# Block transposes by a detour through HBM in a fused attention and SoLU kernel

## The chip, the cores and the metric

The kernel runs on one core of a Trainium2 chip. The metric is the device time of one execution in microseconds; less is better.

## What is computed

Windowed attention over 8 batches and 8 heads of 576 positions with 64 dimensions (a window of 32 for the first four heads, the same reach with a dilation of 4 for the others) gives 4608 rows of 512 numbers. Each row then goes through a layer of two products with a SoLU and a normalisation between them:

```
x = attn_out.transpose(0, 2, 1, 3).reshape(B * S, H * D)      # 4608 x 512
h = x @ w_in                                                  # 4608 x 1024
sm = softmax(h)
solu = h * sm
ln = (solu - mean(solu)) / sqrt(var(solu) + 1e-6) * g_ln
out = ln @ w_out                                              # 4608 x 512
```

## The kernel before

The rows are cut into 36 tiles of 128 tokens. TensorE does both products with operands that are split into a high part and a rest (x_hi and x_lo, th and tl, two parts of each weight), three matmuls for each block of 128: 24 matmuls of 512 columns for the first product of a tile (two halves of 512 columns, L296) and 24 for the second (L378). Attention is done in 32 units of two heads; a unit has scores (S, L188), a softmax on VectorE, GpSimd and ScalarE, a turn by VectorE's 32x32 transposes (L246), and attend (V, L262), whose result is spread into x_hi (ScalarE, L280) and x_lo (VectorE, L283).

For a tile i of the layer the work after the first product is: maximum (peak, VectorE, L307), exponential (e, ScalarE, L314), gate (VectorE, L321, reads the product from PSUM, multiplies with e and sums), centring (mid, VectorE, L333), squares and the scale rstd (var, ScalarE and GpSimd), and then the second product, which needs the activations with their 1024 features on the partitions. So TensorE transposes tile t in eight blocks of 128x128 into two PSUM banks (moe_t, L354), ScalarE casts them to th (L361), VectorE subtracts to get tl (L369). After the second product ScalarE writes ob from PSUM (L388) and SP stores it.

Every engine runs its instructions in the order in which they are written. After an opening that is written out by hand (weights are converted, tiles 0 to 5 of the first product, the first attention units) one loop runs over the tiles, and each step emits the words of STEP in order. A word has a name and says for which index it is meant: i is the step's tile, j the tile before, n and m the attention units of this step and the one before. Step 6 is the first of the loop; steps 12, 21 and 30 to 35 have no new attention unit.

```
STEP = "ha.i hb.i S.n q.n mask.n max.n sub.n hc.i hd.i V.m v.m peak.i exp.n sum.n
        inv.n e.i gate.i mid.i xh.m xl.m var.i norm.n turn.n o.j t.i th.i tl.i out.j"
```

PSUM has eight banks. The first product has banks 0 and 1, once, so the next tile's first product waits for this tile's gate. The second product has bank 2, once, so the next one waits for ob; scores use banks 2 and 3, the transposes 3 and 4, attend 4 to 7. SP issues all transfers: the loads of q, k and v for four units ahead and the stores of the output.

## Time and profile before

| | us |
|---|---|
| median of 3 runs | 568.08 |
| the runs | 568.32, 566.10, 568.08 |
| span of the profiled execution | 564.7 |
| TensorE busy | 529.4 |
| VectorE busy | 358.4 |
| ScalarE busy | 236.4 |
| GpSimd busy | 113.3 |

The span runs from the first to the last instruction of one execution that the profiler recorded on the core. That execution's own time is not listed apart from its span; the three runs lie 1.4 to 3.6 above it, the median 3.4. The transfers move 51.66 MB, 91 GB/s over the span. In the opening TensorE waits for loads and conversions; from about 100 us on it is never idle for long. TensorE's mean granted clock is 0.979 of full speed, and 1.00 in every stretch after the opening.

### The profile page before, as it was taken

To read this page: it belongs to the slowest core of one execution; us is meant where nothing else is said; L and a number is where in the kernel's file an instruction comes from. 1 tells how busy PE (TensorE), PEld (TensorE's weight loads), DVE (VectorE), ACT (ScalarE), POOL (GpSimd) and SP (SyncE) were. 2 spreads that over 40 slices of the span, in tenths; PEclk is the share of its full clock that TensorE was granted. 3 is DMA by queue.
4 is the path that set the end of the run, shared out by engine and by line. 5 is a ranking of instruction groups with operands and counts; after the bars stand their busy time and mean duration, and the time that the engine had idled before them with its cause. 6 is when DMAs were issued, how large, how long until landed. Compare 5 with 4: busy or idle time off the path is not lost.

```text
span 564.7 us, 16571 instructions
## 1 busy us (share of the span) xinstructions
PE 529.4 (94%) x7418; PEld 421.6 (75%) x7418; DVE 358.4 (63%) x554; ACT 236.4 (42%) x384; POOL 113.3 (20%) x258
## 2 busy tenths in 40 slices
PE   3586599999999999999999999999999999999996
PEld 2354477787888888888888888888888888888884
DVE  4778886567666667466667666476667666443431
ACT  4567964543333333433333334433333334432232
POOL 0003662122222222122222221122222221111110
PEclk9867989999999999999999999999999999999999
DMA  8975305222322222112223222123221000000000
GB/s 315 399 283 186 104 1 167 79 79 74 93 93 92 93 93 93 48 64 93 92 93 93 93 92 93 48 64 93 93 93 48 21 21 21 20 24 33 19 20 37
DMA packets 22103, 51.66 MB, mean 91 GB/s; under 512 B 2704, under 2 KB 3088, under 8 KB 22032
## 3 DMA queue, kind: packets, MB, share of 16 engines
q1 hardware_dynamic: 22032, 50.61, 26.6%
q8 instruction: 58, 0.95, 0.7%
q14 instruction: 13, 0.11, 0.1%
HBM read 41.16 MB, written 9.44 MB: 90 GB/s over the span
## 4 chain that ended last, share of the span: by engine, by line
PE 90%; DVE 4%; DMA 3%; ACT 2%; issue 1%; SPq 0%; ACTq 0%
PE banks L296 36%; PE banks L378 35%; PE banks L262 6%; PE banks L354 5%; PE banks L188 5%; PE banks L452 1%; DMA t<-w_in 1%; DMA vt<-vw 1%; DMA mask_sb<-mask 1%; DVE nmax L307 1%; DVE t L321 1%; DVE x_lo L283 0%; PE banks L180 0%; ACT w_i L459 0%; DVE mag L435 0%
## 5 line engine op out<-in xcount | busy, mean ns | idle before, releaser
L296 PE MATMUL banks<-w_i,x_hi 128*128 128x512 f32 x576 | 188.1, 407 | 5.9 <-DVE mu L321 5.6
L378 PE MATMUL banks<-w_o,th 128*128 128x512 f32 x576 | 183.5, 400 | 1.3 <-ACT ob L388 1.3
L296 PEld LDWEIGHTS banks<-w_i,x_hi 128*128 128x128 f32 x576 | 104.9, 191 | 30.4 <-DVE mu L321 6.2
L378 PEld LDWEIGHTS banks<-w_o,th 128*128 128x128 f32 x576 | 106.3, 188 | 25.1 <-ACT ob L388 1.6
L296 PE MATMUL banks<-w_i,x_lo 128*128 128x512 f32 x288 | 114.2, 397 | 0.0
L378 PE MATMUL banks<-w_o,tl 128*128 128x512 f32 x288 | 113.7, 395 | 0.0
L307 DVE TENSOR_REDUCE nmax<-banks 128x1 f32<-128x1024 f32 x36 | 44.0, 1223 | 61.1 <-PE banks L296 61.1
L227 ACT ACTIVATE sm<-sm 128x640 f32<-128x640 f32 x32 | 23.6, 737 | 125.5 <-POOL sm L223 125.5
L369 DVE TENSOR_TENSOR tl<-banks,th 128x512 fp32r<-128x512 f32 x72 | 46.3, 685 | 32.0 <-ACT th L361 31.9
L223 POOL TENSOR_TENSOR sm<-sm,mx 128x640 f32<-128x640 f32 x28 | 35.4, 1263 | 145.9 <-DVE mx L214 140.5
L296 PEld LDWEIGHTS banks<-w_i,x_lo 128*128 128x128 f32 x288 | 54.8, 190 | 12.6
L314 ACT ACTIVATE e<-banks,nmax 128x1024 f32<-128x1024 f32 x36 | 40.2, 1117 | 56.9 <-DVE nmax L307 54.1
L378 PEld LDWEIGHTS banks<-w_o,tl 128*128 128x128 f32 x288 | 54.2, 188 | 12.7
L338 ACT ACTIVATE e<-t 128x1024 f32<-128x1024 f32 x36 | 38.2, 1061 | 53.6 <-DVE t L333 51.2
L202 DVE TENSOR_TENSOR sm<-banks,mask_sb 128x640 f32<-128x640 f32 x28 | 23.1, 824 | 55.3 <-PE banks L188 55.2
L361 ACT CAST th<-banks 128x512 fp32r<-128x512 f32 x72 | 38.7, 589 | 37.8 <-PE banks L354 37.8
L321 DVE CUSTOM_DVE_ANT_0 t<-banks,e 128x1024 f32<-128x1024 f32 x36 | 44.0, 1222 | 14.6 <-ACT e L314 11.7
L262 PEld LDWEIGHTS banks<-pt,vt 32*64 32x64 f32 x2816 | 34.2, 133 | 18.8 <-issue 11.6
L262 PE MATMUL banks<-pt,vt 32*64 32x64 f32 (+3 forms) x2816 | 37.8, 230 | 6.9 <-ACT w_i L459 3.3
L188 PEld LDWEIGHTS banks<-kt,qt 64*32 64x32 f32 x2560 | 29.4, 110 | 17.4 <-issue 15.4
L188 PE MATMUL banks<-kt,qt 64*32 64x64 f32 x2560 | 35.3, 235 | 5.1 <-issue 4.1
L283 DVE TENSOR_TENSOR x_lo<-banks,x_hi 128x576 fp32r<-128x576 f32 x32 | 31.5, 985 | 11.1 <-ACT x_hi L280 11.1
(53 smaller groups left out, 474.2 us busy)
## 6 DMA issues: line engine op xcount, KB each, us to landing
vt<-vw SPq DMA_DIRECT2D x32, 384.0 KB, 3.4
kt<-kT SPq DMA_DIRECT2D x32, 312.0 KB, 3.5
qt<-qT SPq DMA_DIRECT2D x32, 296.0 KB, 4.1
out<-ob SPq DMA_DIRECT2D x36, 256.0 KB, 2.0
t<-w_in SPq DMA_DIRECT2D x6, 512.0 KB, 6.1
t<-w_out SPq DMA_DIRECT2D x4, 512.0 KB, 6.1
raw<-w_out SPq DMA_DIRECT2D x4, 512.0 KB, 5.1
raw<-w_in SPq DMA_DIRECT2D x2, 512.0 KB, 9.1
```

The costliest lines, as they stand in the source:

```text
L188: nc.tensor.matmul(out=ps_s[WIN * c : WIN * c + WIN, h, WQ * i : WQ * i + WQ], lhsT=qt[D * h : D * h + D, q0 : q0 + WIN], rhs=kt[D * h : D ...
L223: eng.tensor_tensor(out=st[n]["sm"], in0=st[n]["sm"], in1=wide(mx), op=ALU.subtract)
L262: nc.tensor.matmul(out=ps_x[D * h : D * h + D, c, c0 : c0 + k1 - k0], lhsT=vt[WIN * c : WIN * c + WIN, i, D * h : D * h + D], rhs=pt[WIN * ...
L283: nc.vector.tensor_tensor(out=x_view(n, x_lo), in0=ps_x, in1=x_view(n, x_hi).bitcast(F32), op=ALU.subtract)
L296: nc.tensor.matmul(out=ps_h[:, half, :], lhsT=a[:, kt, xs], rhs=w_i[:, kt, half, part, :], start=(kt == 0 and k == 0), stop=(kt == KT - 1 ...
L307: nc.vector.tensor_reduce(out=nmax, in_=h, axis=AX.X, op=ALU.max, negate=True)
L314: nc.scalar.activation(out=e, in_=h, func=AF.Exp, bias=nmax, scale=1.0, accum_out=se)
L321: nc.vector.tensor_tensor_reduce(out=t, in0=h, in1=ms[i]["e"], scale=1.0, scalar=0.0, op0=ALU.mult, op1=ALU.add, accum_out=mu,)
L338: nc.scalar.activation(out=e, in_=t, func=AF.Square, accum_out=sq)
L361: nc.scalar.copy(out=th[:, 4 * c : 4 * c + 4], in_=ps_t[c].rearrange("p (f q) -> p f q", q=P))
L369: nc.vector.tensor_tensor(out=tl[:, fs], in0=ps_t[c].rearrange("p (f q) -> p f q", q=P), in1=ms[i]["th"][:, fs].bitcast(F32), op=ALU.subtract,
L378: nc.tensor.matmul(out=ps_o, lhsT=a[:, f, :], rhs=w_o[:, f, part, :], start=(f == 0 and k == 0), stop=(f == FT - 1 and k == 2),)
```

## The change

For the 29 tiles 6 to 34 the eight TensorE transposes are left out. After the centring SP stores tile t into a buffer in HBM by four transfers, one for each group of 32 partitions, in runs of 256 elements (1 KB), so that a row j * 32 + r of the buffer holds, for its row r of each group, the j-th quarter of the features. One transfer reads the buffer back into the tile mv, 4 KB for each partition. In the next step VectorE transposes mv in blocks of 32x32, in two halves of 128x512, back into t; ScalarE casts each half to th, and GpSimd (no longer VectorE) subtracts to get tl. The second product comes two steps behind the first: step i does the second product of tile i-2. Step 6 still does that of tile 5, step 7 does none, and a step is added at the end.

The features come out in another order, so w_out and g_ln are put into that order on the host. The tiles that TensorE still transposes (0 to 5 and 35) get it in their centring, which now writes through a rearranged view into a tile of its own, tp. The program is built with dynamic_dma_scratch_size=4096, where no value was given before.

```diff
-STEP = "ha.i hb.i ... v.m peak.i exp.n sum.n inv.n e.i gate.i mid.i xh.m xl.m var.i norm.n turn.n o.j t.i th.i tl.i out.j"
+STEP = (
+    "back.j ha.i hb.i S.n q.n mask.n max.n sub.n hc.i hd.i V.m v.m peak.i exp.n sum.n inv.n e.i "
+    "tr0.j tr1.j gate.i mid.i forth.i th0.j th1.j tl0.j tl1.j xh.m xl.m var.i norm.n turn.n "
+    "o.k t.i th.i tl.i out.k"
+)
...
     def moe_centre(i):
-        t, mu = ms[i]["t"], ms[i]["mu"]
+        src, dst, mu = ms[i]["t"], ms[i]["t"], ms[i]["mu"]
+        if not by_dma(i):
+            ms[i]["t"] = moe.tile([P, DF], F32, name="tp", bufs=1)
+            dst = ms[i]["t"].rearrange("p (k j s) -> p k j s", j=NG, s=WIN)
+            src = src.rearrange("p (j k s) -> p k j s", j=NG, s=WIN)
...
+    def by_dma(i):
+        return FIRST <= i < LAST
+
+    def move_out(i):
+        mid = ms[i]["dram"] = dram.tile([P, NG, FT * WIN], F32, name="mid")
+        for a in range(NG):
+            nc.sync.dma_start(
+                out=mid.rearrange("(j r) a c -> r j a c", r=WIN)[:, :, a],
+                in_=ms[i]["t"][WIN * a : WIN * a + WIN].rearrange("r (j c) -> r j c", j=NG),
+            )
+
+    def move_back(i):
+        mv = ms[i]["mv"] = moe.tile([P, DF], F32, name=f"raw{4 + i % 2}", bufs=1)
+        nc.sync.dma_start(out=mv, in_=ms[i]["dram"].rearrange("p a c -> p (a c)"))
...
+    def turn_t(i, c):
+        nc.vector.transpose(
+            out=turned(i)[:, half(c)].rearrange("p k (a r) -> p k a r", r=WIN),
+            in_=ms[i]["mv"].rearrange("p (a k s) -> p k a s", a=NG, s=WIN)[:, half(c)],
+        )
+
+    def high_t(i, c):
+        if c == 0:
+            ms[i]["th"] = moe.tile([P, FT, P], F32R, name=f"th{i % TH_BUFS}", bufs=1)
+        nc.scalar.copy(out=ms[i]["th"][:, half(c)], in_=turned(i)[:, half(c)])
+
+    def low_t(i, c):
+        if c == 0:
+            ms[i]["tl"] = moe.tile([P, FT, P], F32R, name=f"tl{i % TH_BUFS}", bufs=1)
+        nc.gpsimd.tensor_tensor(
+            out=ms[i]["tl"][:, half(c)], in0=turned(i)[:, half(c)],
+            in1=ms[i]["th"][:, half(c)].bitcast(F32), op=ALU.subtract,
+        )
...
-    for i in range(FIRST, NTILE + 1):
+    for i in range(FIRST, NTILE + 2):
+        of = {
+            "n": fronts.get(i), "m": fronts.get(i - 1), "i": i, "j": i - 1,
+            "k": {FIRST: FIRST - 1, FIRST + 1: None}.get(i, i - 2),
+        }
```

## The prediction

> **What bounds the kernel now.** I read the page's shares first, then the chain of work that ended last.

> ```profile
> PE 529.4 (94%) x7418; PEld 421.6 (75%) x7418; DVE 358.4 (63%) x554; ACT 236.4 (42%) x384; POOL 113.3 (20%) x258
> PE   3586599999999999999999999999999999999996
> PE 90%; DVE 4%; DMA 3%; ACT 2%; issue 1%; SPq 0%; ACTq 0%
> ```

> TensorE (PE) is busy for 94% of the span and carries 90% of the chain; after the first seven of forty slices it has no gap until the last slice. So a microsecond taken from TensorE's steady stretch should come off the end, as long as nothing else becomes late. The chain in order of time gives the price of the transposes. First a step with attention work, then the last steps without any:

> ```profile
> 154.04 2.78 PE banks L296 x12
> ...
> 295.76 2.77 PE banks L296 x12
> 299.50 2.97 PE banks L296 x12
> 303.47 5.77 PE banks L378 x24
> 310.12 2.77 PE banks L296 x12
> ...
> 529.82 5.51 PE banks L296 x24
> 535.33 5.58 PE banks L378 x24
> 541.78 5.51 PE banks L296 x24
> ```

> The second product (L378) ends at 303.47 + 5.77 = 309.24 and the next first product (L296) begins at 310.12: 0.88 us lies between them, and that is where the eight transposes of L354 run. In the bare steps it is 541.78 - 535.33 - 5.58 = 0.87. Nothing hides it. A step with attention takes 310.12 - 295.76 = 14.4 us, a bare one 541.78 - 529.82 = 12.0; without the transposes 13.5 and 11.1. The mean of the 28 steps from 154.04 to 541.78 is 13.85, since five of them have half of the attention work and four none.

> **What the change removes.** Tiles 6 to 34, 29 tiles, lose the transposes: 29 x 0.87 = **-25.2 us** of TensorE. What has to stay hidden is the rest.

> **VectorE's order.** The page's groups and one tile's timeline:

> ```profile
> L369 DVE TENSOR_TENSOR tl<-banks,th 128x512 fp32r<-128x512 f32 x72 | 46.3, 685 | 32.0 <-ACT th L361 31.9
> L246 DVE STREAM_TRANSPOSE pt<-sm 128x640 f32<-128x640 f32 x32 | 27.0, 843 | 0.8
> L446 ACT CAST w_o<-mag 128x512 fp32r<-128x512 f32 x8 | 4.6, 608 | 0.0
> L461 POOL TENSOR_TENSOR w_o<-mag,w_o x8: 1274/1301/1750, 55.1 to 77.9; 128x512 fp32r<-128x512 f32 x8
> 302.50 1.22 DVE L307 TENSOR_REDUCE nmax<-banks 128x1 f32<-128x1024 f32 x1 [1.15 <-PE banks L296]
> 304.69 0.22 DVE L236 RECIPROCAL rs<-rs 128x10 f32<-128x10 f32 x1
> 305.06 1.23 DVE L321 CUSTOM_DVE_ANT_0 t<-banks,e 128x1024 f32<-128x1024 f32 x1
> 306.20 0.08 DVE L321 DVE_READ_ACCUMULATOR2_ANT mu<- 128x1 f32 x1
> 306.51 0.75 DVE L333 TENSOR_SCALAR t<-t,mu 128x1024 f32<-128x1024 f32 x1
> ```

> VectorE loses two subtractions (2 x 0.685 = 1.37) and gains two block transposes of 512 elements. L246 does 640 in 0.843; a pure ratio gives 0.67, a fixed part like that of L369 gives 0.71. I take 0.71, 1.42 for both: its load stays, but its place moves. Let E be the start of the maximum (302.50). The reciprocal ends at 304.91, the gate now at 306.28. The transposes stand ahead of the gate, so it ends at about 304.95 + 1.42 + 1.31 = 307.7, E+5.2. Behind the gate waits the next first product, because the gate reads its PSUM banks; TensorE gets there when the second product ends, E+6.7. Slack 1.5 us: hidden at no cost, and every microsecond beyond it would cost one. The ScalarE casts now read SBUF, like L446: 0.61 instead of 0.59, nothing. The exact subtractions go to GpSimd at 1.30 each (L461), 2.6 per step on an engine busy for 20%; their result is used a step later.

> **GpSimd beside VectorE.** The casts follow each block transpose, so the two subtractions run at about E+3.9 to E+6.5, and the centring (L333) is ready at E+5.5. The trace has such an overlap while weights are converted:

> ```profile
> 59.64 3.01 POOL L461 TENSOR_TENSOR w_o<-mag,w_o 128x512 fp32r<-128x512 f32 x2
> 60.20 1.29 DVE L427 SCALAR_TENSOR_TENSOR low<-t,low 128x512 int32<-128x512 int32 x1
> 63.85 0.69 DVE L427 SCALAR_TENSOR_TENSOR low<-t,low 128x512 int32<-128x512 int32 x1
> ```

> VectorE's operation takes 1.29 beside GpSimd's and 0.69 nearly alone, so I count the centring as 0 to 1.0 late; in the first case it ends at E+6.25, in the second at E+7.25. From the first block transpose to the end of centring that is T = 1.42 + 1.31 + 0.27 + 0.75 = 3.75, or about 4.8. [...]

> **The detour's time.** SP's order in a step becomes: read back tile i-1, load k and q (behind scores), v (behind attend), four stores of tile i (behind its centring), the output. The read is a new wait, on the four stores. Queued behind it are the loads of k, q and v for four units later, which nobody wants before some 50 us. The stores wait for a centring that ends in mid second product, and behind them stands only the output, due at that product's end: it frees the one ob tile, wanted a step later. So SP's order costs nothing by itself.

> ```profile
> vt<-vw SPq DMA_DIRECT2D x32, 384.0 KB, 3.4
> out<-ob SPq DMA_DIRECT2D x36, 256.0 KB, 2.0
> t<-w_in SPq DMA_DIRECT2D x6, 512.0 KB, 6.1
> 2.10 0.43 SPq L474 DMA_DIRECT2D id_bf<-ident_bf  x1
> 299.52 0.33 SPq L138 DMA_DIRECT2D kt<-kT  x1
> 299.90 1.56 SPq L139 DMA_DIRECT2D qt<-qT  x1
> ```

> A store of 256 KB lands 2.0 after its issue; four of 128 KB at 0.43 each start over 1.3 and land at 3.3. If each following issue takes 1.56, as qt's does here, it is 6.7. The read of 512 KB is not among the quiet rows: at least 3.4 (384 KB), at most 6.1 (among other weight loads); I take 4.0, nearer the quiet row. With 0.1 for each of the two hand-overs the round trip is R = 3.3 + 4.0 + 0.2 = 7.5, between 6.9 and 13.0. Centring, stores, read, block transposes, gate and the next centring form a loop that needs nothing of TensorE but the product: L = R + T = 11.3 to 12.3. Against steps of 13.5 it has room. Against 11.1 it has none.

> **The two ends.** Step 7 has no second product, since o of tile 6 moves to step 8. After its attend (which ends at about E+0.9, where L378 starts in the row at 303.47) TensorE waits for the gate at E+5.2: **+4.3**. What an idle stretch does to TensorE afterwards:

> ```profile
> 65.82 0.39 PE L296 MATMUL banks<-w_i,x_lo 128*128 128x512 f32 x1
> 70.87 1.07 PE L296 MATMUL banks<-w_i,x_hi 128*128 128x512 f32 x2 [4.66 <-DVE mu L321]
> 74.30 0.49 PE L296 MATMUL banks<-w_i,x_lo 128*128 128x512 f32 x1
> ```

> After 4.66 idle the next nine matmuls take 3.7 us to 74.6 instead of 9 x 0.23 = 2.1: 1.6 more. Our gap is a little shorter, so 0 to 1.6; I take **+1.0**. [...]

> The tail, steps 31 to 35, has no attention work:

> ```profile
> 555.05 0.73 PE L378 MATMUL banks<-w_o,th 128*128 128x512 f32 x2 [1.31 <-ACT ob L388]
> 560.50 0.40 PE L378 MATMUL banks<-w_o,tl 128*128 128x512 f32 x1
> 561.07 0.69 ACT L388 ACTIVATE ob<-banks,rstd 128x512 f32<-128x512 f32 x1 [6.07 <-PE banks L378]
> ```

> Today one gap of 1.31 stands ahead of the last second product. After the change two second products follow the last transposes, and the second waits until ob has emptied bank 2: 561.07 + 0.69 - 560.90 is 0.9, about **+1.0**. If the loop is 11.1 or so, that is all. If it is 12.3, the five steps are each 1.2 short; the slack (gate at E+4.0, needed at E+5.6) covers the first two, the next three cost 0.6, 1.2 and 1.3, and in step 35 the last centring is 3.5 late, which delays tile 35's transposes, its casts and ob behind them by some 4.3: 8.4 with the gap. GpSimd starts only about 0.2 ahead of the centring, so either may come first: I take the middle, **+4.7**.

> **Sum.** -25.2 + 4.3 + 1.0 + 4.7 = -15.2, from the span 564.7 to 549.5. The median of the runs, 568.08, lies 3.4 above this span (the lowest 1.4): 552.9 us.

> **Rivals.**
> 1. *All hidden* (loop at most 11.1, no slow matmuls): -25.2 + 4.3 + 1.0 = -19.9, 548.2. For it: short quiet transfers. Against: the stretched row.
> 2. *The detour sets every step* (slower). If R + T passes 13.5, tr waits for the read, the gate behind it waits, and TensorE waits at every tile. With T = 4.8 this begins at R = 8.7. Three issues of 1.56 make R 10.9 and L 15.7: against today's mean of 13.85 that is 29 x 1.85 = +54. With one slow issue in the three R is 8.6 and L 13.4 to 14: the nine shorter steps and the end then lose some 18 and each full step up to 0.5, in all about -2 to +11, 566 to 579. For it: that row. Against: the first issues at 0.43, and a DMA load of only a quarter in this stretch.
> 3. *Slow block transposes*: the view they read and write is broken into runs of 32 elements, where L246 runs over one row. At double the duration the gate ends at E+6.6, still just in time, but T becomes 6.2 and L 13.7: 0.2 lost in each of some 20 full steps (4), up to 2.6 in the nine shorter ones, 14 after their slack: -25.2 + 4.3 + 1.0 + 1.0 + 4 + 14 = -0.9, about 567.

> **Chances.** Forecast 0.62 (549 to 561), all hidden 0.15, detour in every step 0.13, slow transposes 0.10. The range, 546.5 to 561, begins at the all-hidden case less the spread of the runs and leaves out the last two. A measurement of this kernel can tell about 0.5% from no change. Faster by more: the first two and half of the third rival, 0.82; within: 0.08; slower: the second rival's larger part, 0.10.

> **What would show it.** L378 ending directly ahead of L296 in the middle steps (step 13.5); one idle of about 4.3 on TensorE near 165 us, released by VectorE's gate; two gaps at the end; idle of VectorE ahead of the block transposes, released by the DMA of the read, only in the last five steps. If that idle stands in the middle too, the second rival is right. If block transposes take 1.4 us, the third. The forecast falls if middle steps stay at 14.4.

## The result and the profile after

| | before | after |
|---|---|---|
| median, us | 567.09 (4 runs, 565.67 to 568.32) | 549.38 (4 runs, 548.29 to 552.88) |
| profiled execution: span, us | 564.7 | 547.9 (its own time 549.88) |
| TensorE busy, us | 529.4 | 506.0 |

The ratio is 0.9702, with an interval of 0.9666 to 0.9737: the kernel became 3% faster. The changed kernel was run again on another chip: 551.3, ratio 0.9704 (0.9677 to 0.973).

The page's shares, its slices for TensorE with the granted clock, and the shares of the chain, all of the changed kernel:

```profile
PE 506.0 (92%) x7186; PEld 399.3 (73%) x7186; DVE 381.9 (70%) x554; ACT 239.9 (44%) x384; POOL 198.2 (36%) x316
PE   3676779999979999999999999999999999999986
PEclk9867989999997999999999999999999999999999
PE 72%; DVE 11%; DMA 10%; issue 3%; ACT 2%; SPq 1%; DVEq 0%; ACTq 0%
```

TensorE is busy for 23.4 us less. Apart from the opening and the end, two slices differ from the picture before: the twelfth, near 160 us, has a 7 among nines, and in the thirteenth the clock is at 7. That is the step without a second product and what follows it. In the chain, transfers and VectorE now have 21% in place of 7. Read alone, this looks as if the detour had become the bound. The chain in order of time shows where this lies. First the steady stretch, in which only TensorE stands on it:

```profile
175.75 5.77 PE banks L433 x24
181.52 2.72 PE banks L306 x12
...
189.30 5.77 PE banks L433 x24
195.08 2.72 PE banks L306 x12
...
484.14 0.32 SPq L395
...
485.47 2.50 DMA mid<-t
488.10 3.78 DMA raw<-mid
492.10 0.52 DVE t L411
...
494.75 0.77 DVE t L347
```

The second product (L433) ends at 181.52 and the first product (L306) begins at 181.52: the 0.88 us of transposes are gone and nothing took their place. A step is 195.08 - 181.52 = 13.56. The last rows are from the bare steps near the end. There the chain runs through the stores (L395), the read back and VectorE, that is, round the detour's loop, and every step hands on to the next. But TensorE's own timeline has no gap there:

```profile
165.34 1.22 PE L306 MATMUL banks<-w_i,x_hi 128*128 128x512 f32 x2 [3.91 <-DVE mu L331]
...
170.75 1.04 PE L198 MATMUL banks<-kt,qt 64*32 64x64 f32 x80
...
495.43 0.62 PE L306 MATMUL banks<-w_i,x_hi 128*128 128x512 f32 x2
...
506.48 0.62 PE L306 MATMUL banks<-w_i,x_hi 128*128 128x512 f32 x2
...
531.50 0.73 PE L433 MATMUL banks<-w_o,th 128*128 128x512 f32 x2 [1.70 <-ACT ob L443]
...
538.25 0.74 PE L433 MATMUL banks<-w_o,th 128*128 128x512 f32 x2 [0.91 <-ACT ob L443]
```

Bare steps take 506.48 - 495.43 = 11.05. In the second profile of this kernel, on the other chip, the bare steps are as long and the chain gives transfers and VectorE 14% instead of 21. The two gaps at the end are 1.70 and 0.91; before there was one of 1.31. Step by step, from one start of the first product to the next:

| steps | before | after | difference |
|---|---|---|---|
| full attention (most steps) | 14.49 or 14.37 | 13.55 or 13.44 | -0.92 |
| half (12, 13, 21, 22, 30) | 13.14 | 12.22 to 12.27 | -0.9 |
| bare (31 to 34) | 11.95 | 11.05 | -0.9 |
| 7, no second product | 14.37 | 11.79 | |
| 8 | 14.35 | 16.02 | |
| 14 and 23 | 14.49 | 14.18, 14.14 | 0.6 above the other full steps |

From the first matmul of tile 35's first product to the end of the span it is 23.2 before (541.5 to 564.7) and 30.4 after (517.5 to 547.9): 7.2 more, of which 5.6 are one second product that moved there, and 1.6 are waiting.

The balance in the prediction's terms:

| | predicted | measured |
|---|---|---|
| 29 transposes | -25.2 | 29 x -0.92 = -26.7 |
| idle in step 7 | +4.3 | +3.9 |
| slow matmuls after it | +1.0 | +2.5 |
| tail | +4.7 | +1.6 |
| steps 14 and 23 | none | +1.2 |
| up to step 7 | none | +0.7 |
| span | -15.2 | -16.8 |

The opening differs by more than this between two profiles of the changed kernel: tile 6's maximum begins at 146.85 in one and at 148.80 in the other. It is not traced further.

### The profile page after: what moved, and what is told of

It is laid out like the page before. It is cut to its first block, busy times and chain, and to the rows that moved or that the text cites. A ratio compares the mean times of both kernels' runs of the same rounds, so it can differ in the third digit from the quotient of the medians.

```text
span 547.9 us, 16461 instructions
## 1 busy us (share of the span) xinstructions
PE 506.0 (92%) x7186; PEld 399.3 (73%) x7186; DVE 381.9 (70%) x554; ACT 239.9 (44%) x384; POOL 198.2 (36%) x316
## 4 chain that ended last, share of the span: by engine, by line
PE 72%; DVE 11%; DMA 10%; issue 3%; ACT 2%; SPq 1%; DVEq 0%; ACTq 0%
PE banks L306 31%; PE banks L433 28%; PE banks L272 5%; PE banks L198 5%; DMA raw<-mid 4%; DMA mid<-t 3%; DVE t L331 2%; DVE t L347 2%; DVE t L411 2%; DMA raw<-w_in 2%; SPq L395 1%; DVE nmax L317 1%; DMA kt<-kT 1%; PE banks L368 1%; DMA t<-w_in 1%
## 5 line engine op out<-in xcount | busy, mean ns | idle before, releaser
L306 PE MATMUL banks<-w_i,x_hi 128*128 128x512 f32 x576 | 187.0, 406 | 9.8 <-DVE mu L331 9.5
L433 PE MATMUL banks<-w_o,th 128*128 128x512 f32 x576 | 183.6, 400 | 2.6 <-ACT ob L443 2.6
L306 PEld LDWEIGHTS banks<-w_i,x_hi 128*128 128x128 f32 x576 | 108.3, 193 | 36.2 <-DVE mu L331 10.2
L433 PEld LDWEIGHTS banks<-w_o,th 128*128 128x128 f32 x576 | 106.4, 189 | 26.7 <-ACT ob L443 3.3
L424 POOL TENSOR_TENSOR tl<-t,th 128x512 fp32r<-128x512 f32 x58 | 77.0, 1349 | 126.0 <-ACT th L419 126.0
L306 PE MATMUL banks<-w_i,x_lo 128*128 128x512 f32 x288 | 114.7, 398 | 0.0
L433 PE MATMUL banks<-w_o,tl 128*128 128x512 f32 x288 | 113.8, 395 | 0.0
L306 PEld LDWEIGHTS banks<-w_i,x_lo 128*128 128x128 f32 x288 | 55.4, 192 | 12.4
L433 PEld LDWEIGHTS banks<-w_o,tl 128*128 128x128 f32 x288 | 54.3, 189 | 12.7
L352 ACT ACTIVATE e<-t 128x1024 f32<-128x1024 f32 x29 | 30.8, 1062 | 52.5 <-DVE t L347 52.5
L347 DVE TENSOR_SCALAR t<-t,mu 128x1024 f32<-128x1024 f32 x29 | 48.1, 1659 | 1.0
L198 PEld LDWEIGHTS banks<-kt,qt 64*32 64x32 f32 x2560 | 29.3, 110 | 19.9 <-issue 15.6
L331 DVE CUSTOM_DVE_ANT_0 t<-banks,e 128x1024 f32<-128x1024 f32 x36 | 42.9, 1192 | 0.6 <-ACT e L324 0.3
L411 DVE STREAM_TRANSPOSE t<-raw 128x512 f32<-128x512 f32 x58 | 37.8, 690 | 5.4 <-DMA raw<-mid 5.3
## 6 DMA issues: line engine op xcount, KB each, us to landing
raw<-mid SPq DMA_DIRECT2D x29, 512.0 KB, 3.6
vt<-vw SPq DMA_DIRECT2D x32, 384.0 KB, 3.9
out<-ob SPq DMA_DIRECT2D x36, 256.0 KB, 2.6
t<-w_in SPq DMA_DIRECT2D x6, 512.0 KB, 6.1
t<-w_out SPq DMA_DIRECT2D x4, 512.0 KB, 6.4
```

The costliest lines, as they stand in the source:

```text
L198: nc.tensor.matmul(out=ps_s[WIN * c : WIN * c + WIN, h, WQ * i : WQ * i + WQ], lhsT=qt[D * h : D * h + D, q0 : q0 + WIN], rhs=kt[D * h : D ...
L306: nc.tensor.matmul(out=ps_h[:, half, :], lhsT=a[:, kt, xs], rhs=w_i[:, kt, half, part, :], start=(kt == 0 and k == 0), stop=(kt == KT - 1 ...
L331: nc.vector.tensor_tensor_reduce(out=t, in0=h, in1=ms[i]["e"], scale=1.0, scalar=0.0, op0=ALU.mult, op1=ALU.add, accum_out=mu,)
L347: nc.vector.tensor_scalar(out=dst, in0=src, scalar1=mu, scalar2=None, op0=ALU.subtract)
L352: nc.scalar.activation(out=e, in_=t, func=AF.Square, accum_out=sq)
L411: nc.vector.transpose(out=turned(i)[:, half(c)].rearrange("p k (a r) -> p k a r", r=WIN), in_=ms[i]["mv"].rearrange("p (a k s) -> p k a s" ...
```

## The experiments

Where a ratio is given, it is against the kernel before on the same chip (medians 568.16, 568.29 and 567.63), with its interval.

**Is the gain the transposes, and what does the order alone cost?** The order of two steps stays, TensorE transposes every tile:

```diff
     def by_dma(i):
-        return FIRST <= i < LAST
+        return False
```

> The order of the changed kernel (second product two steps behind, none in step 7, a step more at the end), but TensorE transposes every tile and nothing goes through HBM. If the gain is the 0.88 us of transposes per tile, this keeps all costs and has no gain: 3.8 idle in step 7 (TensorE waits for the centring of tile 7), about 2.6 of slow matmuls behind it, 1 to 2 at the end, so 6 to 8 over before, about 574. If the gain comes from the second product standing later, it is near the changed kernel, 550.

Measured 574.63, ratio 1.0121 (1.0094 to 1.0147). In TensorE's timeline of this run the idle stretch is there, and full and bare steps are back at 14.49 and 11.95:

```profile
165.34 2.27 PE L368 MATMUL banks<-id_sb,tp 128*128 128x128 f32 x8 [3.85 <-DVE tp L347]
```

So the second product two steps behind costs some 6.5 us by itself, and the transposes' removal brings 24 to 25 beside it (the ratio falls from 1.0121 to 0.9702, the times from 574.63 to 549.38 on two chips). This run keeps dynamic_dma_scratch_size=4096, too, so that value is not what shortens the steps.

**Is the detour hidden?** Stores and read are left out; the block transposes read the centred tile itself.

```diff
-    "back.j ha.i hb.i S.n ... e.i "
-    "tr0.j tr1.j gate.i mid.i forth.i th0.j ... "
+    "ha.i hb.i S.n ... e.i "
+    "tr0.j tr1.j gate.i mid.i th0.j ... "
...
-            in_=ms[i]["mv"].rearrange("p (a k s) -> p k a s", a=NG, s=WIN)[:, half(c)],
+            in_=ms[i]["src"].rearrange("p (a k s) -> p k a s", a=NG, s=WIN)[:, half(c)],
```

> Leaves out the stores to HBM and the read back: the block transposes take the centred tile itself, so the features of a tile are not exchanged between groups of partitions and the output is another one; all other instructions stay. If the detour is wholly hidden, the time is that of the changed kernel within 1 us (549), and the middle steps stay at 13.5. If its traffic or the wait for the read costs something, it is faster by that: 0.4 us per step would give 538.

Measured 550.17, ratio 0.9678 (0.9642 to 0.9713): no difference from the changed kernel. All steps are as long as there, but for 14 and 23 (13.56 instead of 14.18 and 14.14) and step 8 (14.94). From tile 35's first product to the end it is 29.9 instead of 30.4, and the first gap there is 1.39 instead of 1.70. So the transfers are hidden but for at most some 1.8 us, those 1.2 and some 0.6 at the end. Step 8 shows that the price of an idle stretch varies: 3.77 idle, and of the 24 matmuls behind it only the first seven are slow.

**What does the empty step cost?** Twelve matmuls of tile 5's second product are repeated in step 7, and their result isn't read.

```diff
+    def moe_again():
+        th, tl = again
+        for f in range(FT // 2):
+            for k, (a, part) in enumerate(((th, 0), (th, 1), (tl, 0))):
+                nc.tensor.matmul(
+                    out=ps_o, lhsT=a[:, f, :], rhs=w_o[:, f, part, :],
...
+                if word == "o.k" and i == FIRST + 1:
+                    moe_again()
```

> In step 7, which has no second product, half of the second product of tile 5 is done once more into bank 2 and never read (12 matmuls, 2.8 us). If idle TensorE is what makes the matmuls after it slow, the idle falls from 3.9 to about 1.1, the first 12 matmuls of step 8 take 2.8 instead of 5.4, and the time falls by 2.6 to about 546.8. If they are slow for another reason, nothing changes, 549.4.

Measured 547.32, ratio 0.9638 (0.9612 to 0.9663). TensorE's timeline of this run:

```profile
163.38 0.73 PE L306 MATMUL banks<-w_i,x_hi 128*128 128x512 f32 x2 [0.93 <-DVE mu L331]
```

Useless work in the gap makes the kernel faster: step 7 keeps its length (11.74), but step 8 takes 13.57 instead of 16.02. The 2.5 us behind the idle stretch are the price of the idleness itself, and the idleness is VectorE's gate, which takes its time anyway.

**Gate ahead of the block transposes.**

```diff
-    "tr0.j tr1.j gate.i mid.i forth.i th0.j th1.j ... "
+    "gate.i mid.i forth.i tr0.j tr1.j th0.j th1.j ... "
```

> The gate, the centring and the stores come ahead of the block transposes of the tile before, on VectorE and on SP. The idle in step 7 falls by the two transposes, 1.3, to 2.6. If slow matmuls need a longer idle than that, another 2.6 goes: 545.5. If they come anyway, 548. If the block transposes, now later, hold up the next step's mask, the middle steps grow over 13.5 and the gain is lost.

Measured 550.54, ratio 0.97 (0.9676 to 0.9724), 2.5 to 5 above what was expected. TensorE's timeline of this run:

```profile
163.56 1.22 PE L306 MATMUL banks<-w_i,x_hi 128*128 128x512 f32 x2 [2.87 <-DVE mu L331]
...
530.69 0.73 PE L433 MATMUL banks<-w_o,th 128*128 128x512 f32 x2 [2.97 <-ACT ob L443]
...
532.22 1.05 PE L433 MATMUL banks<-w_o,th 128*128 128x512 f32 x2
```

Step 7 is 1.1 shorter, but behind 2.87 of idleness the matmuls are still slow: the first pair takes 1.22. And at the end the casts of tile 34, now late, stand ahead of ob on ScalarE: a gap of 2.97 and slow matmuls again, the pair 1.05 instead of 0.62. The next second product starts 539.00 - 530.69 = 8.31 later instead of 6.75. What was gained early was given back late, and step 9 is 0.7 longer.

**How far is the detour from the bound?** Each store is issued twice.

```diff
-        for a in range(NG):
+        for a in 2 * list(range(NG)):
```

> Each of the four stores is issued a second time into the same buffer and waits for the first to land, so the round trip from centring to the read's landing grows by about 3 us, from 7.3 to 10.3; nothing else changes. If the detour is a loop hidden under the step only as long as round trip and VectorE's part (3.4 to 4.5) fit into it, the loop is now 13.7 to 14.8: every bare step (11.05 now) grows to that, full steps (13.55) to a little over 14, and the time rises to 565 to 600, about 575. If the detour is hidden with several us to spare, the time stays at 549 to 551.

Measured 623.87, ratio 1.0973 (1.0917 to 1.1028): more than any theory said. Waits on TensorE, the chain's shares, and one step in the timelines of SP and VectorE of this run:

```profile
PE banks L306 <- DVE mu L331: 47.7, 29, 4.7
```

```profile
DMA 45%; DVE 20%; PE 20%; SPq 6%; issue 6%; ACT 2%; DVEq 0%; ACTq 0%
```

```profile
344.98 4.50 SPq L395 DMA_DIRECT2D mid<-t  x8
...
352.09 0.34 SPq L402 DMA_DIRECT2D raw<-mid  x1
...
355.57 1.30 DVE L411 STREAM_TRANSPOSE t<-raw 128x512 f32<-128x512 f32 x2 [2.31 <-DMA raw<-mid]
...
358.22 1.87 DVE L347 TENSOR_SCALAR t<-t,mu 128x1024 f32<-128x1024 f32 x1
```

From the first store at 344.98 to the block transposes at 355.57 it is 10.6 us, and about 11 in most other steps, where 10.3 was expected. VectorE waits for the read, the gate behind it is late, and TensorE waits for the gate 29 times. Steps 9 to 29 take 14.7 to 16.5, bare ones 13.5 to 14.2. This is the rival in which the detour sets every step, brought about by the edit. T, from the block transposes to the end of the centring (358.22 + 1.87 = 360.09), is 4.5 in this step, and 10.6 + 4.5 = 15.1 against 13.5. Some 3 us more of round trip put some 2 on each step, so that the room was about 1.

**Does GpSimd's part pay?** The subtractions go back to VectorE.

```diff
-        nc.gpsimd.tensor_tensor(
+        nc.vector.tensor_tensor(
```

> The two exact subtractions of a tile run on VectorE instead of GpSimd, in the same place of the order. VectorE gains 1.37 per step and its centring, with no GpSimd operation beside it, should fall from 1.89 to 0.75 in the full steps. If the stretched centring is contention with GpSimd, the two nearly cancel and the time is 549 within 1.5. If VectorE is near its limit, the middle steps grow over 13.55 by some tenths each, 552 to 560.

Measured 550.09, ratio 0.9663 (0.9612 to 0.9715): the same as the changed kernel. The centring of the 29 tiles in this run, by line (durations in ns: min/median/max):

```profile
L347 DVE TENSOR_SCALAR t<-t,mu x29: 752/753/757, 156.0 to 520.4; 128x1024 f32<-128x1024 f32 x29
```

The same line in the changed kernel:

```profile
L347 DVE TENSOR_SCALAR t<-t,mu x29: 753/1889/1908, 150.9 to 516.3; 128x1024 f32<-128x1024 f32 x29
```

With the subtractions off GpSimd no centring takes longer than 0.757. The same holds in the run with the gate first, where the centring stands ahead of GpSimd's subtractions: all 29 take 0.75. So the 1.89 is the subtractions' doing, and the move to GpSimd, 2 x 0.685 us less for VectorE in each step, is given back by 1.14 more for the centring. Neither shows in the time, since TensorE sets the full steps at 13.55 in both kernels. Steps 14 and 23 are at 13.58 here, too.

**The end of the program.** ScalarE writes ob ahead of the last casts and squares, and tile 35's second product has a bank of its own.

```diff
-    "tr0.j ... xh.m xl.m var.i norm.n turn.n "
-    "o.k t.i th.i tl.i out.k"
+    "tr0.j ... xh.m xl.m norm.n turn.n "
+    "o.k t.i out.k th.i tl.i var.i"
...
+    def o_bank(i):
+        return banks[:, 5, :] if i == LAST else ps_o
```

> ScalarE empties bank 2 (ob) ahead of the last casts and of the squares, and the second product of tile 35 goes to bank 5. If the gaps ahead of the last two second products are waits for ob, both go (1.7 and 0.9), and so do the two waits of scores for ob in steps 14 and 23 (0.6 each): 3.8 less, 545.6. If the squares, now later, hold up the exponential of the next tile, the middle steps grow.

Measured 546.03, ratio 0.9616 (0.9571 to 0.966). The last rows of the chain in this run:

```profile
526.91 1.09 PE banks L368 x8
528.00 11.16 PE banks L436 x48
```

Both second products (48 matmuls) run without a gap; from tile 35's first product to the end it is 27.6 instead of 30.4.

**Both together, twice.** The first attempt had the end's order, the gate first in step 7 alone, the scores of step 8 moved into step 7, and six smaller repeated matmuls behind them.

```diff
+                    out=banks[:, 7, 160:416], lhsT=a[:, f, :], rhs=w_o[:, f, part, 0:256],
...
+        if i == FIRST + 1:
+            words_i.remove("gate.i")
+            words_i.insert(words_i.index("tr0.j"), "gate.i")
...
+                if word == "o.k" and i == FIRST + 1:
+                    scores(fronts[i + 1])
+                    moe_again()
```

> The edits of the run before, and step 7 filled: its gate ahead of the block transposes, the scores of step 8 done in it, and six matmuls of 256 columns whose result nobody reads, so that TensorE has no idle stretch over 1 us there. The idle falls from 3.9 to about 1 with 1.0 of it now real work, slow matmuls (2.5) go, the ends lose 3.8: about 8.5 less than the changed kernel, 541. If the slow matmuls come anyway, 543.5.

Measured 549.24, ratio 0.9675 (0.963 to 0.972): nothing left of the end's gain. TensorE's timeline of this run:

```profile
167.93 0.80 PE L448 MATMUL banks<-w_o,th 128*128 128x256 f32 x2 [6.06 <-DVE x_lo L293]
```

The repeated matmuls wrote to bank 7, which VectorE was still reading for x_lo: the filling waited 6.06 us itself and brought a longer idle stretch than the one it was to fill. The second attempt repeats three full matmuls into bank 2, the second product's own, ahead of the scores:

```diff
-                    out=banks[:, 7, 160:416], lhsT=a[:, f, :], rhs=w_o[:, f, part, 0:256],
+                    out=ps_o, lhsT=a[:, f, :], rhs=w_o[:, f, part, :],
...
                 if word == "o.k" and i == FIRST + 1:
-                    scores(fronts[i + 1])
-                    moe_again()
+                    moe_again()
+                    scores(fronts[i + 1])
```

> As the run best, but the idle stretch of step 7 is filled in an order that waits for nothing: three matmuls of tile 5's second product, done again into bank 2, then the scores of step 8. Against the changed kernel the idle falls from 3.9 to about 1, of it 1.0 real work taken from step 8, slow matmuls (2.5) go if they come from the idle, the ends give 3.4: 7 to 8 less, 542. If the slow matmuls come anyway, 544.5.

Measured 543.28 (6 runs), ratio 0.958 (0.9548 to 0.9611). TensorE's timeline of this run:

```profile
164.29 0.73 PE L306 MATMUL banks<-w_i,x_hi 128*128 128x512 f32 x2 [1.01 <-DVE mu L331]
```

Its median ratio is the lowest of all versions, though its interval overlaps with that of the end's order alone (0.9571 to 0.966). The gate and the scores add little to the filling: from step 7's first product to step 10's it is 38.6 us here and 38.9 with the filling alone, since new small waits (0.26 to 0.62) appear in steps 8 and 9.

The changed kernel itself, unedited, on that chip:

> The changed kernel itself, unedited, for a comparison on the same chip: 549.4 within 1.5.

Measured 551.3, ratio 0.9704 (0.9677 to 0.973); step 8 takes 16.24 and steps 14 and 23 take 14.18, much as in the first profile. The time is 0.4 above the range that was expected; the ratio is the same as the first (0.9702).

## Why the prediction held

Predicted were 552.9 us, and 549.38 were measured. The mechanism was right: TensorE's steady stretch sets the time, the transposes were exposed in it, and the way round them is hidden but for at most 1.8 us. That the number is so close is in part luck. The tail, the transposes and the idle stretch came out 3.1, 1.5 and 0.4 lower than their terms, the slow matmuls, steps 14 and 23 and the stretch up to step 7 1.5, 1.2 and 0.7 higher: errors of 5.0 and 3.4 leave 1.6. The measured time lies nearer to the first rival (548.2) than to the forecast. Of that rival's two conditions the one on the loop held in its effect, since the bare steps stayed at 11.05, and the other, no slow matmuls, did not. Point by point:

**The transposes.** 0.87 each was read from the gap between the second product and the next first one. A step lost 0.92. The first half of the first product is itself 0.05 shorter, 2.72 in the chain against 2.77, now that it follows large matmuls and not the transposes. 29 x 0.05 = 1.5 us of gain lay outside the gap that was measured.

**VectorE's order.** The groups, issues and waits of the changed kernel:

```profile
L424 POOL TENSOR_TENSOR tl<-t,th 128x512 fp32r<-128x512 f32 x58 | 77.0, 1349 | 126.0 <-ACT th L419 126.0
L411 DVE STREAM_TRANSPOSE t<-raw 128x512 f32<-128x512 f32 x58 | 37.8, 690 | 5.4 <-DMA raw<-mid 5.3
mid<-t SPq DMA_DIRECT2D x116, 128.0 KB, 2.4
raw<-mid SPq DMA_DIRECT2D x29, 512.0 KB, 3.6
```

Block transposes take 0.69 each (0.71 predicted): the third rival, slow transposes, falls. The pair takes 1.30, and in a full step the gate ends at E+4.8 where E+5.2 was expected and E+6.7 would still have been early enough.

**The detour.** One full and one bare step in the timelines of VectorE, GpSimd, SP and ScalarE of the changed kernel, with the one wait that was not foreseen:

```profile
246.08 1.88 DVE L347 TENSOR_SCALAR t<-t,mu 128x1024 f32<-128x1024 f32 x1
248.06 1.06 ACT L352 ACTIVATE e<-t 128x1024 f32<-128x1024 f32 x1 [2.66 <-DVE t L347]
249.12 0.67 ACT L443 ACTIVATE ob<-banks,rstd 128x512 f32<-128x512 f32 x1
249.84 1.04 PE L198 MATMUL banks<-kt,qt 64*32 64x64 f32 x80 [0.53 <-ACT ob L443]
...
284.88 2.55 POOL L424 TENSOR_TENSOR tl<-t,th 128x512 fp32r<-128x512 f32 x2 [3.72 <-ACT th L419]
286.09 1.89 DVE L347 TENSOR_SCALAR t<-t,mu 128x1024 f32<-128x1024 f32 x1
...
483.36 0.75 DVE L347 TENSOR_SCALAR t<-t,mu 128x1024 f32<-128x1024 f32 x1
484.14 1.76 SPq L395 DMA_DIRECT2D mid<-t  x4
488.10 0.34 SPq L402 DMA_DIRECT2D raw<-mid  x1
492.10 1.30 DVE L411 STREAM_TRANSPOSE t<-raw 128x512 f32<-128x512 f32 x2 [0.83 <-DMA raw<-mid]
...
493.60 3.06 POOL L424 TENSOR_TENSOR tl<-t,th 128x512 fp32r<-128x512 f32 x2 [6.21 <-ACT th L419]
494.75 0.75 DVE L347 TENSOR_SCALAR t<-t,mu 128x1024 f32<-128x1024 f32 x1
```

From the end of the centring (483.36 + 0.75 = 484.11) to the block transposes at 492.10 it is 8.0 us in this step, 7.2 to 8.2 in the other six in which VectorE waits; R = 7.5 was predicted. In the other steps the read lands 7.2 to 9.0 behind the centring, mostly some 1 us before VectorE comes to it. VectorE waits for the read in only those seven steps, 5.3 us in all, those with half or none of the attention work, and in none of them does TensorE wait behind it. The second rival didn't come about. With the doubled stores it did, and its own threshold, R = 8.7 at T = 4.8, is about 1 us away from most steps, and single steps reach it.

**The tail** is the term that was mis-sized most: +4.7 taken, 1.6 measured, near the lower end of its range (1.0). The step that failed is "GpSimd starts only about 0.2 ahead of the centring, so either may come first: I take the middle". GpSimd starts earlier than that, 1.0 to 1.2 ahead in every step from 7 on, and still the centring has two lengths: that the first to start comes first was the author's estimate, and no run shows it. In a full step the pair begins at 284.88 and the centring at 286.09, 1.21 later: the centring takes 1.89 and the pair 2.55. In a bare step they begin at 493.60 and 494.75, 1.15 later: now the centring takes 0.75 and GpSimd's pair 3.06. Where one is long, the other is short; which of the operations went ahead the recorded starts don't show, since by them the centring is ahead of the second subtraction in both, by 0.04 and 0.10. In 23 of the 25 steps 6 to 30 the centring takes 1.85 to 1.91 and begins 1.21 behind GpSimd's start. Step 6 has no subtraction on GpSimd, and in step 25 the centring began 1.21 behind, too, and took 0.75, so that both lengths occur at 1.21. In the four bare steps it begins 1.02 to 1.15 behind and takes 0.75 to 0.83. The second profile of the changed kernel and the one with the doubled stores show the same split: 1.85 to 1.90 at 1.20 to 1.22, and 0.75 to 0.83 at 1.02 to 1.16. So T in a bare step is 494.75 + 0.77 - 492.10 = 3.4, and the loop, from one centring to the next, is 494.75 - 483.36 = 11.4, 10.6 and 10.9 in the next two: about a bare step, as in the forecast's better case. It rests on some 0.06 us in the offset of two engines, 1.15 against 1.21.

**The empty step.** The idle stretch was 3.91 (4.3 predicted). The slow matmuls behind it cost 2.5 (1.0 predicted, at most 1.6): mis-sized, since the only example in the trace of before was taken for the upper end. The windows of the changed kernel, the first two in the idle stretch (columns: length, then busy time of PE, PEld, DVE, ACT and POOL with their instructions, granted clock, DMA share, GB/s):

```profile
161.50:163.80 2.30, 0.00 (x0) 0.00 (x0) 2.23 (x6) 1.41 (x3) 0.00 (x0) 1.00 0.54 174
163.95:165.30 1.35, 0.00 (x0) 0.00 (x0) 1.33 (x3) 1.35 (x3) 1.01 (x1) 0.50 0.00 0
165.30:170.70 5.40, 5.36 (x12) 3.80 (x12) 4.73 (x5) 1.77 (x3) 3.85 (x8) 0.50 0.39 97
170.75:174.00 3.25, 3.25 (x91) 2.78 (x91) 1.65 (x2) 0.00 (x0) 0.34 (x1) 1.00 0.52 165
```

Twelve matmuls run for 5.4 us at half the clock: 0.45 for each, where 0.23 is usual. The clock fell while TensorE was still idle, and full speed returns with the scores at 170.75. Without the transfers, behind 3.77 of idleness, the half clock ends much sooner:

```profile
169.00:171.95 2.95, 2.95 (x7) 2.37 (x8) 2.91 (x3) 1.41 (x2) 2.44 (x5) 0.50 0.00 0
172.00:175.00 3.00, 3.00 (x89) 2.29 (x89) 2.34 (x4) 0.26 (x2) 1.37 (x3) 1.00 0.02 5
```

So the price is about half of what is left of the half clock when the matmuls begin: 5.4 us of it cost 2.5 in one run and 3.0 cost 1.4 in the other. What the traces show of its length stands in the last section.

**What was missed.** Steps 14 and 23 lose 0.6 each. The rows near 246 to 250 show how: in step 13, without an attend, the centring ends late (1.88), the squares on ScalarE (L352) wait for it, ob (L443) stands behind them, and the scores of step 14 need ob's bank. It was not among the steps of the prediction: VectorE's late centring was followed to TensorE's transposes and to SP, but not to ob behind the squares. It is gone where the subtractions are on VectorE, and nearly so (13.78 and 13.56) with ob ahead of the squares. Without the transfers it is gone too, since there the centring of these two steps falls on the quick side (0.75); what shifts it there was not traced.

**From span to time.** 3.4 was added for the median above the span. In each run after, 1.9 to 2.0 lie between span and time, and 1.8 in the later runs of the kernel before; the rest of the 3.4 was that the profiled execution of before was a quick one. Of the 3.5 us by which the forecast was too high, 1.6 are in the span, 1.4 in this term, and 0.5 are the profiled execution above its median.

## What to carry to other kernels

When an engine sets the end without a gap, work that is moved off it counts in full (here 0.92 us for each of 29 tiles, of which the gap showed 0.87), and a chain of 12 us through four other engines and HBM costs next to nothing (here at most 1.8 us in all) as long as it is shorter than a step; find by doubling one part of it how near it is. A chain of waits that runs through a transfer is no proof that the transfer bounds: look for the gap on the busy engine first. A step that is left without work at a change of order costs its idleness, here 3.91 us, and here up to 2.5 us again in slow matmuls, so put something into it, and see that the filling doesn't wait itself.

## What the runs showed of the hardware

How much idleness brought slow matmuls is less sharp. Behind 0.93 us (twelve repeated matmuls), 1.01 (three) and 1.70 (the end of the changed kernel, clock 1.00) the first pair took 0.73. Behind 2.87 (the gate first) and 3.91 (the changed kernel) it took 1.22. The step lost 1.4 us behind 3.77 (without the transfers) and 2.5 behind 3.91.
